# The first attention-scale group of a DiT block: one added by a ones matmul, four VectorE products straight from PSUM, and a new order of the opening

## The chip, the cores and the metric

The kernel runs on one core of a Trainium2 chip. The metric is the device time of one execution in microseconds. Before the change it is 243.63 us, the median of five runs (243.14 to 243.85). All window times below count from the first instruction of the profiled execution.

## The reference

A diffusion-transformer block on 2 batches of 256 tokens with 1152 features. A conditioning vector `c` gives six modulation vectors; the layer-normed input is scaled and shifted, goes through attention with two heads, is gated and added back, and then the same is done around an MLP.

```python
mod = (_silu(c) @ w_mod).reshape(B, 6, 1, D)
shift_a, scale_a, gate_a, shift_m, scale_m, gate_m = [mod[:, i] for i in range(6)]
h = _layernorm(x, axis=-1) * (1 + scale_a) + shift_a
qkv = (h @ wqkv).reshape(B, N, 3, H, Dh)
q, k, v = (qkv[:, :, 0].copy(), qkv[:, :, 1].copy(), qkv[:, :, 2].copy())
attn = _softmax(jnp.einsum('bqhd,bkhd->bhqk', q, k) * Dh ** (-0.5), axis=-1)
a = jnp.einsum('bhqk,bkhd->bqhd', attn, v).reshape(B, N, D) @ wo
x = x + gate_a * a
h2 = _layernorm(x, axis=-1) * (1 + scale_m) + shift_m
m = _gelu(h2 @ w_fc1) @ w_fc2
return x + gate_m * m
```

The change concerns only `(1 + scale_a)` and the product with the layer-normed `x`.

## The kernel before

The 512 tokens are four token tiles of 128 (tiles 0 and 1 are batch 0, tiles 2 and 3 batch 1). The 1152 features are nine chunks of 128, counted by `k`. Activations that feed a matmul lie transposed, features on partitions, tokens along the free dimension: `hT0[:, k, tokens]` (in the trace it is part of `big`). The K projection is built first, chunk by chunk: `k_step(k, c0, c1)` (L288) multiplies chunk `k` of the tokens `c0` to `c1` with six column blocks of `w_k`, one matmul each, and adds into six PSUM accumulators `pk`. A step on one token tile is six matmuls with 128 columns, on two tiles six with 256, on all tiles six with 512.

What a step needs comes through four engines:

- VectorE gathers the statistics of a token tile (`stats_piece`, L188 and L193; for tile 1 ScalarE does it, L203), ScalarE takes the square root (`sqrt1`, L219), VectorE the reciprocal (`recip1`, L222) and then normalizes the tile in two pieces (`norm1`, L235): columns up to CUT = 512, which are the first four chunks, and the other 640 later. The result is `xn`.
- TensorE transposes 128x128 blocks of `xn` into PSUM tiles `pt` (L266 in `transpose_x`, L358 in `transpose_into`).
- The scale comes by `scale_group(g)`: the loads of the scale columns are split into four groups, KGROUPS = chunks 0-1, 2-3, 4-5 and 6-8. For each chunk nine matmuls (L248) with two columns, one for each batch, add up in a PSUM tile `pm`. `add_one` then writes `scale_a` to SBUF with one added, on VectorE (L256) or ScalarE (L258, with the tile `one_t` as bias).
- `modulate` multiplies a transposed block in PSUM with its chunk's scale, read per partition from SBUF, and writes `hT0`, on VectorE (L273) or ScalarE (L275). The shift is added later.

The tiles `pc`, `pt` and `pm` take turns in two PSUM banks, so a new one waits until the earlier content of its bank has been read. Every engine works through its instructions in the order in which the Python code issues them: the last loop of the kernel ties each instruction to the one before it on its engine. So the opening is a schedule written out by hand. `warm(n, pwarm)` (L171) issues matmuls on zeros whose result nobody reads. SyncE issues all loads in one queue: `x`, then in turn a scale group and the chunks of `w_k` that belong to it, then the other weights. In the profiled execution the last packet of scale group 0 lands at 8.85 us, of `w_k` chunk 0 at 9.37, chunk 1 at 9.95, scale group 1 at 11.94, `w_k` chunk 2 at 12.46 and chunk 3 at 13.02.

The opening's order on TensorE around the change is: transposes of tile 0's chunks 0 and 1, four warm matmuls, the 18 scale matmuls of group 0, one warm matmul, six transposes (tile 1's chunks 0 and 1, chunks 2 and 3 of both tiles), `k_step` 0 and 1 on tile 0 and then on tile 1, two transposes of tile 2, the 18 scale matmuls of group 1, `k_step` 0 and 1 on tile 2, `k_step` 2 on tiles 0 and 1. ScalarE scales tile 0's two chunks and later tile 2's; VectorE scales tile 1's, and chunks 2 and 3 of tiles 0 and 1.

Of the kernel before, what the change touches and what calls it, by code (L numbers as in the profile page):

```python
# [8 lines left out]
FP32 = mybir.dt.float32  # L9
BF16 = mybir.dt.bfloat16  # L10
ACT = mybir.ActivationFunctionType
# [8 lines left out]
def kernel(  # L20
# [11 lines left out]
    nc = tc.nc  # L32
    B, N, D = x.shape
# [3 lines left out]
    P = 128  # L37
    T = B * N
    NT = T // P
    TPB = N // P  # L40
    KD = D // P
# [3 lines left out]
    NPD = D // PW  # L45
# [6 lines left out]
    const = ctx.enter_context(tc.tile_pool(name="const", bufs=1))  # L52
# [6 lines left out]
    def acc_tile(shape, name, dt=FP32):  # L59
        return psum.tile(shape, dt, name=name, tag="acc", bufs=6)  # L60

    def aux_tile(shape, name, dt=FP32):
        return psum.tile(shape, dt, name=name, tag="aux", bufs=2)
# [25 lines left out]
    ident = const.tile([P, P], BF16, name="ident")  # L89
    make_identity(nc, ident[:])  # L90
    eps_t = const.tile([P, 1], FP32, name="eps_t")
    nc.vector.memset(eps_t[:], LN_EPS)  # L92
    one_t = const.tile([P, 1], FP32, name="one_t")
    nc.vector.memset(one_t[:], 1.0)
    SW = 32
    sT = act.tile([P, KD, SW], BF16, name="sT")
    nc.gpsimd.memset(sT[:], 0.0)
# [1 line left out]
    KGROUPS = [(0, 2), (2, 4), (4, 6), (6, 9)]  # L99
# [59 lines left out]
    hT0 = aT  # L159
# [9 lines left out]
    def warm(n, dst):  # L169
        for _ in range(n):  # L170
            nc.tensor.matmul(dst[:], zeros[:, 0:P], zeros[:], start=True, stop=True)  # L171
# [12 lines left out]
    xns = [work.tile([P, D], BF16, name="xn", tag="xn", bufs=4) for _ in range(NT)]  # L184
    stats1 = [small.tile([P, NPD, 6], FP32, name="stats1", tag="stats1") for _ in range(NT)]

    def stats_piece(t, j, aggregate=True):
        nc.vector.bn_stats(stats1[t][:, j, :], x_sb[:, t, j * PW:(j + 1) * PW])  # L188
        if j == NPD - 1 and aggregate:
            stats_aggregate(t)  # L190

    def stats_aggregate(t):
        nc.vector.bn_aggr(mv1[:, t, :], stats1[t][:].rearrange("p a b -> p (a b)"))  # L193
# [24 lines left out]
    def sqrt1(t):  # L218
        nc.scalar.activation(rstd1[:, t:t + 1], mv1[:, t, 1:2], ACT.Sqrt, bias=eps_t[:], scale=1.0)  # L219

    def recip1(t, with_nb=False):
        nc.vector.reciprocal(rstd1[:, t:t + 1], rstd1[:, t:t + 1])  # L222
        if with_nb:
            nc.vector.scalar_tensor_tensor(
                nb1[:, t:t + 1], mv1[:, t, 0:1], -1.0, rstd1[:, t:t + 1], op0=ALU.mult, op1=ALU.mult
            )

    def norm1(t, c0, c1, eng):
        if eng == "a":
            nc.scalar.activation(  # L230
                xns[t][:, c0:c1], x_sb[:, t, c0:c1], ACT.Identity,
                bias=nb1[:, t:t + 1], scale=rstd1[:, t:t + 1],
            )
        else:
            nc.vector.tensor_scalar(  # L235
                xns[t][:, c0:c1], x_sb[:, t, c0:c1], mv1[:, t, 0:1], rstd1[:, t:t + 1],
                op0=ALU.subtract, op1=ALU.mult,
            )


    scale_a = act.tile([P, KD, B], FP32, name="scale_a")

    def scale_group(g):
        k0, k1 = KGROUPS[g]
        pm = aux_tile([P, k1 - k0, B], "pm")
        for j in range(k0, k1):
            for k in range(KD):
                nc.tensor.matmul(  # L248
                    pm[:, j - k0, :], w_scale_a[:, k, j * P:(j + 1) * P], sT[:, k, 0:B],
                    start=(k == 0), stop=(k == KD - 1),  # L250
                )

        def add_one(eng):
            dst = scale_a[:, k0:k1, :]
            if eng == "d":
                nc.vector.tensor_scalar_add(dst, pm[:], 1.0)  # L256
            else:
                nc.scalar.activation(dst, pm[:], ACT.Identity, bias=one_t[:])  # L258

        return add_one  # L260

    def transpose_x(ks, ts, pt=None, js=None):
        pt = aux_tile([P, len(ks), len(ts) * P], "pt", BF16) if pt is None else pt
        for i, k in enumerate(ks):
            for j, t in enumerate(ts) if js is None else zip(js, ts):
                nc.tensor.transpose(pt[:, i, j * P:(j + 1) * P], xns[t][:, k * P:(k + 1) * P], ident[:])  # L266
        return pt

    def modulate(pt, i, k, t0, j0, w, eng):
        b = t0 // TPB  # L270
        dst, src, sc = hT0[:, k, t0 * P:t0 * P + w], pt[:, i, j0:j0 + w], scale_a[:, k, b:b + 1]
        if eng == "d":
            nc.vector.tensor_scalar_mul(dst, src, sc)  # L273
        else:
            nc.scalar.mul(dst, src, sc)  # L275
# [8 lines left out]
    def k_step(k, c0=0, c1=T, m0=0, m1=KM1):  # L284
        for m in range(m0, m1):
            if k == 0 and c0 == 0:
                pk[m] = acc_tile([P, T], "pk")
            nc.tensor.matmul(  # L288
                pk[m][:, c0:c1], w_k[:, k, m * P:(m + 1) * P], hT0[:, k, c0:c1],
                start=(k == 0 and c0 == 0), stop=(k == KD - 1), skip_group_check=True,  # L290
            )
# [39 lines left out]
    CUT = 4 * P  # L331
# [7 lines left out]
    recip1(0)  # L339
    norm1(0, 0, CUT, "d")  # L340
    stats_piece(2, 1)
    pt_0 = transpose_x([0, 1], [0])
    warm(4, pwarm)
    act_stats_finish()
    sqrt1(T_ACT)
# [1 line left out]
    recip1(1)  # L347
    norm1(1, 0, CUT, "d")
    stats_aggregate(2)
    norm1(0, CUT, D, "d")  # L350
    scale_group(0)("a")
    for k in range(2):
        modulate(pt_0, k, k, 0, 0, P, "a")
    warm(1, pwarm)
    pt_1 = aux_tile([P, 1, 8 * P], "pt", BF16)

    def transpose_into(pt, slot, k, t):
        nc.tensor.transpose(pt[:, 0, slot * P:(slot + 1) * P], xns[t][:, k * P:(k + 1) * P], ident[:])  # L358

    for k in range(2):  # L360
        transpose_into(pt_1, k, k, 1)
    for k in (2, 3):
        for t in range(TPB):
            transpose_into(pt_1, 2 * (k - 1) + t, k, t)
    for k in range(2):
        modulate(pt_1, 0, k, 1, k * P, P, "d")
    sqrt1(2)
    k_step(0, 0, P)
    k_step(1, 0, P)
    stats_piece(3, 0)  # L370
    recip1(2)
    norm1(2, 0, CUT, "d")
    k_step(0, P, N)
    k_step(1, P, N)
    stats_piece(3, 1)
    stats_piece(3, 2)
    for k in range(2):
        transpose_into(pt_1, 6 + k, k, 2)
    for k in range(2):
        modulate(pt_1, 0, k, 2, (6 + k) * P, P, "a")  # L380
    scale_group(1)("a")
    sqrt1(3)
    for k in (2, 3):
        modulate(pt_1, 0, k, 0, 2 * (k - 1) * P, N, "d")
    k_step(0, N, N + P)
    k_step(1, N, N + P)
    recip1(3)
    norm1(3, 0, CUT, "d")
    k_step(2, 0, N)
    k_step(3, 0, N, 0, 3)  # L390
    pt_4 = transpose_x([0, 1], [3])
    for k in range(2):
        modulate(pt_4, k, k, 3, 0, P, "d")
    k_step(3, 0, N, 3, KM1)
    norm1(1, CUT, D, "d")
    pt_5 = transpose_x([2, 3], [2, 3])
    for i, k in enumerate((2, 3)):
        modulate(pt_5, i, k, 2, 0, N, "a")
    norm1(2, CUT, D, "d")
    norm1(3, CUT, D, "d")  # L400
    add2 = scale_group(2)
    k_step(0, N + P, T)
    k_step(1, N + P, T)
# [46 lines left out]
    for k in range(KD):  # L450
        for b in range(B):
            dst, src = hT[:, k, b * N:(b + 1) * N], hT0[:, k, b * N:(b + 1) * N]
# [56 lines left out]
    for k in range(KD):  # L509
        for m in range(KM1):  # L510
            nc.tensor.matmul(  # L511
                pq[m][:], w_q[:, k, m * P:(m + 1) * P], hT[:, k, :],
                start=(k == 0), stop=(k == KD - 1),
            )
    for m in range(KD):
        if m >= KM1:
            pq.append(acc_tile([P, T], "pacc"))
            for k in range(KD):
                nc.tensor.matmul(
                    pq[m][:], w_q[:, k, m * P:(m + 1) * P], hT[:, k, :],  # L520
                    start=(k == 0), stop=(k == KD - 1),
# [10 lines left out]
    for b in range(B):  # L532
        for h in range(H):
            scores[b, h] = acc_tile([P, TPB, N], "ps_s")
            for qt in range(TPB):
                q0 = b * N + qt * P
                for i in range(HC):
# [3 lines left out]
                        start=(qt == 0 and i == 0), stop=False, skip_group_check=True,  # L541
                    )
    for b in range(B):
        for qt in range(TPB):
            q0 = b * N + qt * P
            for h in range(H):
# [3 lines left out]
                    start=False, stop=True, skip_group_check=True, tile_position=(h * HP, 0),  # L550
# [309 lines left out]
    for gi, (n, t, c0, cw) in enumerate(groups):  # L860
        b = t // TPB
        last = gi == len(groups) - 1
        pacc = acc_tile([P, cw], "pacc")
        for kk in range(KF):
            j, r = divmod(n * KF + kk, 27)
# [3 lines left out]
                start=(kk == 0), stop=(kk == KF - 1),  # L869
# [11 lines left out]
    for ins in list(nc.cur_bb.bb.instructions)[first_traced:]:  # L881
        eng = ins.engine
# [38 lines left out]
```

## Time and profile before

| | |
|---|---|
| device time of the profiled execution | 243.63 us |
| its span, first to last instruction | 241.9 us |
| median of five runs | 243.63 us |
| granted TensorE clock, mean | 1.000 |
| 0 to 9.85 us | TensorE busy 8.41, VectorE 5.12, ScalarE 6.46 us |
| 9.85 to 15.80 us | TensorE busy 5.69, VectorE 4.67, ScalarE 2.25 us |
| 15.80 to 33.50 us | TensorE busy 17.56, VectorE 6.62, ScalarE 4.84 us |
| 33.50 to 98.60 us | TensorE busy 64.88, VectorE 40.59, ScalarE 29.67 us |
| 98.60 us to the end | TensorE busy 139.85, VectorE 36.41, ScalarE 26.29 us |

The page gives busy time and share of each engine (PE is TensorE's matmuls, PEld its weight loads, DVE VectorE, ACT ScalarE, POOL GpSimd, SP SyncE, a q behind the name its sequencer). A line of the timeline gives the start, the duration from the first start to the last end, engine, line, operation, output and input, shape and count of a run of equal instructions, and in brackets the idle time before them and what ended it. The duration of a TensorE matmul counts to its modelled end, which lies behind the start of the next one; how fast matmuls follow each other is read from their starts.

### The profile page before, as it was taken

Reading aid. Unit: us, or ns where it says so; the run is one execution under the profiler, and the core shown is the slowest. Engines: PE = TensorE matmul, PEld = TensorE weight load, DVE = VectorE, ACT = ScalarE, POOL = GpSimd, SP = SyncE. Lnnn points to the kernel's source line nnn. Section 1 sums busy time; section 2 is a strip of 40 time slices with the busy share of each in tenths; the row PEclk is TensorE's granted clock in tenths of the full one; section 3 lists DMA queues with packets and bytes.
Section 4 is the critical chain, followed back from the end, with each engine's and each line's share of the span. In section 5 each row is a group of like instructions: output and inputs, shape, how many; then the busy total and the mean of one; then the engine's idle time right before and its main releaser. Section 6 shows DMA issues by size and latency. Waiting matters only on the chain.

```text
span 241.9 us, 4031 instructions
## 1 busy us (share of the span) xinstructions
PE 236.4 (98%) x1698; PEld 143.1 (59%) x1698; DVE 93.4 (39%) x209; ACT 69.5 (29%) x138; POOL 31.9 (13%) x48
## 2 busy tenths in 40 slices
PE   8999999999999999999999999999999999999994
PEld 2595444466656666888844444444666566665673
DVE  3772450665694676620000029999002000000001
ACT  6532240543736074782222233322000000000000
POOL 1000400000310616200000000000314111111111
PEclk9999999999999999999999999999999999999999
DMA  6999999999999999799999999995891000000000
GB/s 230 322 332 360 378 345 245 339 368 280 253 323 362 379 253 211 202 211 327 328 327 260 200 289 328 326 326 164 264 273 33 19 16 16 20 21 26 18 19 16
DMA packets 76989, 54.48 MB, mean 225 GB/s; under 512 B 26011, under 2 KB 72491, under 8 KB 76971
## 3 DMA queue, kind: packets, MB, share of 16 engines
q1 hardware_dynamic: 76240, 53.02, 77.5%
q0 software_dynamic: 704, 1.20, 1.6%
q8 instruction: 13, 0.21, 0.4%
q14 instruction: 5, 0.04, 0.1%
q10 hardware_dynamic: 27, 0.00, 0.0%
HBM read 46.90 MB, written 1.19 MB: 199 GB/s over the span
## 4 chain that ended last, share of the span: by engine, by line
PE 58%; ACT 2%; DMA 1%; issue 0%; DVE 0%; ACTq 0%; DVEq 0%
PE pacc L866 29%; PE pacc L802 29%; ACT hT L687 2%; DMA hT<-xn 1%; ACT xn L666 0%; ACT rstd L657 0%; DVE tmp L872 0%; DVE o_sb L874 0%; ACTq L687 0%; DVEq L872 0%
## 5 line engine op out<-in xcount | busy, mean ns | idle before, releaser
L802 PE MATMUL pacc<-hT,w_f 128*128 128x256 bf16 (+1 forms) x432 | 70.5, 326 | 0.2 <-ACT hT L687 0.2
L866 PE MATMUL pacc<-w_f,gT 128*128 128x384 bf16 (+2 forms) x468 | 70.5, 314 | 0.0
L866 PEld LDWEIGHTS <-gT 128*128 128x128 bf16 x468 | 44.4, 98 | 26.3
L802 PEld LDWEIGHTS <-w_f 128*128 128x128 bf16 x432 | 42.2, 98 | 28.1 <-issue 0.4
L485 DVE SCALAR_TENSOR_TENSOR late<-w_gate_mT,late 128x1152 bf16<-128x1152 bf16 x18 | 24.4, 1357 | 36.2 <-DMA w_gate_mT<-in_w_mod_dram 35.7
L872 DVE TENSOR_TENSOR tmp<-pacc,gate 128x384 f32<-128x384 f32 (+2 forms) x13 | 6.8, 526 | 62.7 <-PE pacc L866 50.8
L840 ACT ACTIVATE gT<-pacc 128x512 bf16<-128x512 f32 x24 | 14.3, 597 | 32.3 <-PE pacc L802 32.3
L485 DVE SCALAR_TENSOR_TENSOR s_spill<-w_scale_m,s_b 128x1152 bf16<-128x1152 bf16 x12 | 16.3, 1357 | 8.6 <-DMA w_scale_m<-in_w_mod_dram 8.2
L874 POOL TENSOR_TENSOR o_sb<-tmp,x 128x384 bf16<-128x384 f32 (+1 forms) x12 | 11.6, 973 | 47.7 <-DVE tmp L872 47.7
L705 PE MATMUL pacc<-w_o,big 128*128 128x384 bf16 (+2 forms) x117 | 17.9, 314 | 0.0
L584 PE MATMUL pacc<-w_v,hT 128*128 128x384 bf16 x108 | 17.9, 326 | 0.0
L705 PEld LDWEIGHTS <-big 128*128 128x128 bf16 x117 | 11.0, 98 | 6.8 <-ACT big L627 0.2
L584 PEld LDWEIGHTS <-hT 128*128 128x128 bf16 x108 | 10.4, 98 | 7.0 <-issue 0.2
L288 PE MATMUL pk<-big,w_k 128*128 128x128 bf16 (+2 forms) x102 | 13.3, 279 | 0.0
L711 POOL TENSOR_TENSOR x<-tmp,x_sb 128x384 f32<-128x384 f32 (+1 forms) x11 | 9.8, 888 | 17.4 <-DVE tmp L710 9.6
L511 PE MATMUL pacc<-hT,w_q 128*128 128x512 bf16 x54 | 11.8, 379 | 0.1
L327 POOL DMA_DIRECT2D gates_dram<-grow x4 | 2.1, 519 | 70.6 <-DVE grow L826 70.6
L818 ACT ACTIVATE gT<-pacc 128x512 bf16<-128x512 f32 x12 | 6.9, 595 | 10.3 <-PE pacc L802 10.2
L288 PEld LDWEIGHTS <-w_k 128*128 128x128 bf16 x102 | 7.7, 98 | 3.0
L511 PEld LDWEIGHTS <-w_q 128*128 128x128 bf16 x54 | 5.3, 98 | 6.7 <-issue 0.4
L171 PE MATMUL pwarm<-zeros 128*128 128x512 bf16 x21 | 7.9, 533 | 1.2 <-DVE eps_t L92 1.2
L710 DVE TENSOR_TENSOR tmp<-pacc,gate 128x384 f32<-128x384 f32 (+2 forms) x13 | 6.7, 522 | 5.4 <-PE pacc L705 5.2
(101 smaller groups left out, 159.4 us busy)
## 6 DMA issues: line engine op xcount, KB each, us to landing
w_f<-in_w_fc_dram SPq DMA_DIRECT2D x14, 864.0 KB, 10.9
w_f<-in_w_fc_dram SPq DMA_DIRECT2D x2, 2592.0 KB, 10.5
w_f<-in_w_fc_dram SPq DMA_DIRECT2D x2, 1728.0 KB, 13.7
w_shift_a<-in_w_mod_dram SPq DMA_DIRECT2D x3, 864.0 KB, 10.6
w_v<-in_wqkv_dram SPq DMA_DIRECT2D x3, 864.0 KB, 6.0
w_gate_a<-in_w_mod_dram SPq DMA_DIRECT2D x3, 864.0 KB, 9.2
w_o<-in_wo_dram SPq DMA_DIRECT2D x3, 864.0 KB, 6.1
w_shift_m<-in_w_mod_dram SPq DMA_DIRECT2D x3, 864.0 KB, 13.0
```

The source lines that it names most:

```text
L171: nc.tensor.matmul(dst[:], zeros[:, 0:P], zeros[:], start=True, stop=True)
L288: nc.tensor.matmul(pk[m][:, c0:c1], w_k[:, k, m * P:(m + 1) * P], hT0[:, k, c0:c1], start=(k == 0 and c0 == 0), stop=(k == KD - 1), skip_g ...
L485: nc.vector.scalar_tensor_tensor(spill, wT[:, j, :], 1.0, s_b[b], op0=ALU.mult, op1=ALU.mult, accum_out=dst(j, b),)
L511: nc.tensor.matmul(pq[m][:], w_q[:, k, m * P:(m + 1) * P], hT[:, k, :], start=(k == 0), stop=(k == KD - 1),)
L584: nc.tensor.matmul(pacc[:], hT[:, k, t * P:(t + 1) * P], w_v[:, k, pnl * PW:(pnl + 1) * PW], start=(k == 0), stop=(k == KD - 1),)
L705: nc.tensor.matmul(pacc[:], aT[:, k, t * P:(t + 1) * P], w_o[:, k, c0:c1], start=(k == ks[0]), stop=(k == ks[-1]),)
L711: (nc.vector if (t, i) in ((1, 2), (3, 3)) else nc.gpsimd).tensor_tensor(x1[:, t, c0:c1], tmp[:], x_sb[:, t, c0:c1], op=ALU.add)
L802: nc.tensor.matmul(dst, w_f1[m // KD][:, k, ml * P:(ml + 1) * P], hT[:, k, c0:c1], start=(k == 0), stop=(k == KD - 1),)
L818: nc.scalar.activation(gT[:, ms[0]:ms[-1] + 1, b * N:(b + 1) * N], pacc[:], ACT.Gelu_apprx_tanh)
L840: nc.scalar.activation(gT[:, m, :], pacc[:], ACT.Gelu_apprx_tanh)
L866: nc.tensor.matmul(pacc[:], gT[:, kk, t * P:(t + 1) * P], w_f2[j][:, r, c0 - n * PW:c0 - n * PW + cw], start=(kk == 0), stop=(kk == KF - 1),)
L874: (nc.vector if last else nc.gpsimd).tensor_tensor(o_sb[:], tmp[:], x1[:, t, c0:c0 + cw], op=ALU.add)
```

## The change

- `one_t` goes. A row of 128 ones (`ones_r`, one partition, bf16) takes its place.
- `scale_group` is split in `scale_group_matmuls` and `scale_group_copy`. The matmuls of each of the four groups are headed by one matmul of `ones_r` with itself, which sets every sum in `pm` to one; the scale matmuls add to it, so none of them starts a sum. What reads `pm` is then a plain copy.
- For group 0, tile 0's and tile 1's transposed chunks 0 and 1 lie in one PSUM tile `pt_0`, and VectorE makes all four products, with the scale read straight from `pm_0` in PSUM. ScalarE copies `pm_0` to `scale_a` for later use by batch 1.
- The order of the opening changes. Tile 1's two transposes follow the group-0 scale matmuls at once. The square root of tile 2 is taken before the copy; VectorE normalizes tile 2 right behind the four products and takes the statistics of tile 3 behind that in one piece. The four transposes of chunks 2 and 3 stand between `k_step` 0 and 1 on tile 1. The group-1 scale matmuls move from before to behind `k_step(0)` on tile 2, and `k_step(1)` on tile 2 follows them. ScalarE instead of VectorE scales chunks 2 and 3 of tiles 0 and 1, with tile 3's square root between the two. VectorE normalizes the rest of tile 0 (`norm1(0, CUT, D)`) later, in front of the same piece of tile 1.

```diff
-    one_t = const.tile([P, 1], FP32, name="one_t")
-    nc.vector.memset(one_t[:], 1.0)
+    ones_r = const.tile([1, P], BF16, name="ones_r")
+    nc.vector.memset(ones_r[:], 1.0)
...
-    def scale_group(g):
+    def scale_group_matmuls(g):
         k0, k1 = KGROUPS[g]
         pm = aux_tile([P, k1 - k0, B], "pm")
+        nc.tensor.matmul(
+            pm[:].rearrange("p j b -> p (j b)"), ones_r[:, 0:P], ones_r[:, 0:(k1 - k0) * B], start=True, stop=False,
+            skip_group_check=True,
+        )
         for j in range(k0, k1):
             for k in range(KD):
                 nc.tensor.matmul(
                     pm[:, j - k0, :], w_scale_a[:, k, j * P:(j + 1) * P], sT[:, k, 0:B],
-                    start=(k == 0), stop=(k == KD - 1),
+                    start=False, stop=(k == KD - 1), skip_group_check=True,
                 )
 
-        def add_one(eng):
+        return pm
+
+    def scale_group_copy(g, pm):
+        k0, k1 = KGROUPS[g]
+
+        def copy_out(eng):
             dst = scale_a[:, k0:k1, :]
             if eng == "d":
-                nc.vector.tensor_scalar_add(dst, pm[:], 1.0)
+                nc.vector.tensor_copy(dst, pm[:])
             else:
-                nc.scalar.activation(dst, pm[:], ACT.Identity, bias=one_t[:])
...
+    def scale_group(g):
+        return scale_group_copy(g, scale_group_matmuls(g))
...
-    pt_0 = transpose_x([0, 1], [0])
+    def transpose_into(pt, slot, k, t):
+        nc.tensor.transpose(pt[:, slot * P:(slot + 1) * P], xns[t][:, k * P:(k + 1) * P], ident[:])
+
+    pt_0 = aux_tile([P, 4 * P], "pt", BF16)
+    for k in range(2):
+        transpose_into(pt_0, k, k, 0)
     warm(4, pwarm)
...
     stats_aggregate(2)
-    norm1(0, CUT, D, "d")
-    scale_group(0)("a")
+    sqrt1(2)
+    pm_0 = scale_group_matmuls(0)
     for k in range(2):
-        modulate(pt_0, k, k, 0, 0, P, "a")
+        transpose_into(pt_0, 2 + k, k, 1)
+    for t in range(TPB):
+        for k in range(2):
+            nc.vector.tensor_scalar_mul(
+                hT0[:, k, t * P:(t + 1) * P], pt_0[:, (2 * t + k) * P:(2 * t + k + 1) * P], pm_0[:, k, 0:1]
+            )
+    nc.scalar.copy(scale_a[:, 0:2, :], pm_0[:])
     warm(1, pwarm)
-    pt_1 = aux_tile([P, 1, 8 * P], "pt", BF16)
...
-    for k in range(2):
-        transpose_into(pt_1, k, k, 1)
+    recip1(2)
+    norm1(2, 0, CUT, "d")
+    pt_1 = aux_tile([P, 8 * P], "pt", BF16)
+    k_step(0, 0, P)
+    k_step(1, 0, P)
+    for j in range(NPD):
+        stats_piece(3, j)
+    k_step(0, P, N)
     for k in (2, 3):
         for t in range(TPB):
             transpose_into(pt_1, 2 * (k - 1) + t, k, t)
-    for k in range(2):
-        modulate(pt_1, 0, k, 1, k * P, P, "d")
-    sqrt1(2)
-    k_step(0, 0, P)
-    k_step(1, 0, P)
-    stats_piece(3, 0)
-    recip1(2)
-    norm1(2, 0, CUT, "d")
-    k_step(0, P, N)
     k_step(1, P, N)
-    stats_piece(3, 1)
-    stats_piece(3, 2)
     for k in range(2):
         transpose_into(pt_1, 6 + k, k, 2)
     for k in range(2):
-        modulate(pt_1, 0, k, 2, (6 + k) * P, P, "a")
-    scale_group(1)("a")
-    sqrt1(3)
+        nc.scalar.mul(hT0[:, k, N:N + P], pt_1[:, (6 + k) * P:(7 + k) * P], scale_a[:, k, 1:2])
+    k_step(0, N, N + P)
+    pm_1 = scale_group_matmuls(1)
+    nc.scalar.copy(scale_a[:, 2:4, :], pm_1[:])
     for k in (2, 3):
-        modulate(pt_1, 0, k, 0, 2 * (k - 1) * P, N, "d")
-    k_step(0, N, N + P)
-    k_step(1, N, N + P)
+        nc.scalar.mul(hT0[:, k, 0:N], pt_1[:, 2 * (k - 1) * P:2 * k * P], scale_a[:, k, 0:1])
+        if k == 2:
+            sqrt1(3)
     recip1(3)
     norm1(3, 0, CUT, "d")
+    k_step(1, N, N + P)
     k_step(2, 0, N)
     k_step(3, 0, N, 0, 3)
     pt_4 = transpose_x([0, 1], [3])
     for k in range(2):
         modulate(pt_4, k, k, 3, 0, P, "d")
     k_step(3, 0, N, 3, KM1)
+    norm1(0, CUT, D, "d")
     norm1(1, CUT, D, "d")
```

More of the change, by code (lines that the diff above doesn't have):

```diff
@@ L249, in scale_group @@
                     pm[:, j - k0, :], w_scale_a[:, k, j * P:(j + 1) * P], sT[:, k, 0:B],
-                    start=(k == 0), stop=(k == KD - 1),
+                    start=False, stop=(k == KD - 1), skip_group_check=True,
                 )
-        def add_one(eng):
+        return pm
+    def scale_group_copy(g, pm):
+        k0, k1 = KGROUPS[g]
+        def copy_out(eng):
             dst = scale_a[:, k0:k1, :]
             if eng == "d":
-                nc.vector.tensor_scalar_add(dst, pm[:], 1.0)
+                nc.vector.tensor_copy(dst, pm[:])
             else:
-                nc.scalar.activation(dst, pm[:], ACT.Identity, bias=one_t[:])
-        return add_one
+                nc.scalar.copy(dst, pm[:])
+        return copy_out
+    def scale_group(g):
+        return scale_group_copy(g, scale_group_matmuls(g))
     def transpose_x(ks, ts, pt=None, js=None):
@@ L349 @@
     stats_aggregate(2)
-    norm1(0, CUT, D, "d")
-    scale_group(0)("a")
+    sqrt1(2)
+    pm_0 = scale_group_matmuls(0)
     for k in range(2):
-        modulate(pt_0, k, k, 0, 0, P, "a")
-    warm(1, pwarm)
-    pt_1 = aux_tile([P, 1, 8 * P], "pt", BF16)
-    def transpose_into(pt, slot, k, t):
-        nc.tensor.transpose(pt[:, 0, slot * P:(slot + 1) * P], xns[t][:, k * P:(k + 1) * P], ident[:])
-    for k in range(2):
-        transpose_into(pt_1, k, k, 1)
+        transpose_into(pt_0, 2 + k, k, 1)
[5 more added lines that the diff above has]
+    nc.scalar.copy(scale_a[:, 0:2, :], pm_0[:])
+    warm(1, pwarm)
+    recip1(2)
[6 more added lines that the diff above has]
+    k_step(0, P, N)
     for k in (2, 3):
```

## The prediction

> **What bounds the kernel now.** I read the page's first two parts, then the waits, then the timeline, first from 0 to 14 us and then in slices narrow enough to show single matmuls.
>
> ```profile
> PE 236.4 (98%) x1698; PEld 143.1 (59%) x1698; DVE 93.4 (39%) x209; ACT 69.5 (29%) x138; POOL 31.9 (13%) x48
> ...
> PEclk9999999999999999999999999999999999999999
> ```
>
> TensorE is the bound. Busy time hides short stalls, because a matmul's pipelined tail counts as busy, so I compare starts: neighbouring 128-column matmuls start 0.056 us apart (24 of them from 10.25 to 11.59), 256-column ones 0.109, the 2-column scale matmuls 0.025. What starts later than that is a stall.
>
> ```profile
> 8.89 0.60 PE L248 MATMUL pm<-sT,w_scale_a 128*128 128x2 bf16 x18
> 9.54 0.26 ACT L258 ACTIVATE scale_a<-pm,one_t 128x4 f32<-128x4 f32 x1 [1.27 <-PE pm L248]
> 9.83 0.62 ACT L275 ACTIVATE big<-pt,scale_a 128x128 bf16<-128x128 bf16 x2
> 9.85 0.49 PE L358 MATMUL pt<-ident,xn 128*128 128x128 bf16 x6
> 10.25 1.50 PE L288 MATMUL pk<-big,w_k 128*128 128x128 bf16 x24
> 11.50 0.41 DVE L235 TENSOR_SCALAR xn<-x_sb,mv,rstd 128x512 bf16<-128x512 bf16 x1
> 11.97 0.28 PE L358 MATMUL pt<-ident,xn 128*128 128x128 bf16 x2 [0.22 <-DVE xn L235]
> 12.09 0.59 PE L248 MATMUL pm<-sT,w_scale_a 128*128 128x2 bf16 x18
> 12.29 0.62 ACT L275 ACTIVATE big<-pt,scale_a 128x128 bf16<-128x128 bf16 x2 [1.65 <-PE pt L358]
> ```
>
> The reader is to see two chains. At 9.54 ScalarE adds one, scales, and lets the K matmuls start at 10.25. At 12.29 it scales token tile 2 while TensorE works through the 18 scale matmuls of group 1, placed there as filler. By starts, TensorE's stalls from 9.36 to 13.51 are 0.27 (before 9.85), 0.07 (10.25), 0.38 (11.97, waiting for VectorE's norm), 0.17 (12.71) and 0.13 (before the 256-wide step at 13.51): 1.02 us in all. After 16 us the only stalls over 0.1 us are 0.30 at 33.48 and 0.38 at 98.56; both end chains that TensorE's own results start (the waits name ScalarE L687 for the second, never a load). So later stages move with TensorE, and a us here is a us at the end.
>
> **What the Trainium skill says.** "TensorEngine Tiling (Array Packing)", Key Properties: changing the tiling mode drains TensorE. The ones matmul contracts over one row, so it is built with a 32-row tile, between 128-row ones. The trace agrees where a 64-row tile is entered and left:
>
> ```profile
> 54.34 0.27 PE L539 MATMUL ps_s<-big 128*128 128x256 bf16 x1
> 54.54 0.39 PE L548 MATMUL ps_s<-big 64*128 64x256 bf16 x4
> ```
>
> From 54.34 to 54.54 is 0.205 where 0.109 is normal: 0.095 lost on entry, and again on leaving (54.88 to 55.09). The one small row-tile there is, the transpose of c, agrees for the exit:
>
> ```profile
> 3.01 0.19 PE L174 MATMUL pc<-ident,c_sb 18*128 18x18 bf16 x1
> 3.13 0.61 PE L171 MATMUL pwarm<-zeros 128*128 128x512 bf16 x1
> ```
>
> "VectorE: DVE Perf Modes", Scalar operands, allows a per-partition scalar operand and names no extra price; no row of before has one in PSUM. "PSUM — Partial Sum Buffer", PSUM bank collisions, says two engines must not touch one bank at once; so ScalarE's copy out of the scale's bank is made to wait for VectorE's four products. It has over 1 us to spare.
>
> **The change, part by part.** I follow TensorE's order in the changed program.
>
> (1) Head. The ones matmul of group 0 sits in the stall before the load's arrival at 8.89: nothing (0.1 if leaving its tile costs after the load has landed). The 18 end at 9.36; tile 1's two transposes follow at 9.36 and 9.42, and the last ends at 9.42+0.22=9.64 (xn of tile 1 is ready at 8.98). VectorE starts 0.04 later, as it does after L266 (14.54+0.22 to 14.80). Its 0.38 us norm of tile 0's tail, which ran at 9.04, has moved away. First product 9.68 to 9.96, K matmuls 0.05 later (as from 11.91 to the load at 11.96): 10.01 instead of 10.25, **−0.24**. The products come every 0.20 us (L273), the matmuls of one step take 0.33, so none waits again. The PSUM scalar: at least 0, at most 0.10 (half a step); I take 0.
>
> (2) Tile 2 comes earlier. VectorE is free at 10.48 and sqrt1(2) has run; reciprocal 0.18, norm 0.41: 11.07, not 11.91. TensorE does 24 matmuls (1.34) and four transposes (0.22): tile 2's transposes at 11.57 instead of 11.97, **−0.40** by here.
>
> (3) The filler is gone. Group 1's scale matmuls now stand behind k_step(0,N,N+P). The second transpose ends at 11.63+0.22=11.85; ScalarE starts 0.10 later (this wait goes through an extra semaphore instruction, as 15.31 to 15.41), and from its start to the matmul takes 0.42 (12.29 to 12.71): 12.37. TensorE was free at 11.69, so a **0.68 us stall** replaces 0.38+0.17.
>
> (4) k_step(0,N,N+P) to 12.70. Then the ones matmul: 0.095 in, 0.025, 0.095 out, that is **0.215**; nothing covers it. The 18 from 12.92 to 13.37, k_step(1,N,N+P) to 13.70. Their result goes through ScalarE in series, copy and then the 256-wide product. Before, from the last scale matmul's start (9.34) to the product's start (9.83) was 0.49: 13.34+0.49=13.83. To the matmul 0.42, plus 0.11 for 256 columns (0.48 against 0.37): 14.36. A **0.66 us stall**, where before VectorE's product let the step start at 13.51. k_step(2,0,N) is now 0.85 late. Check by stalls: now 0.32 (before 10.01), 0.68, 0.66 and 0.19 for the switches, 1.85 against 1.02, plus 0.025 of matmul: 0.85.
>
> (5) The rest. The second product starts 0.37+0.25 after the first (sqrt1(3) between), ends near 14.92 and is in time for 15.01. pm_2's ones matmul waits for VectorE anyway (0.18 at 15.33): entry hidden, 0.12 added, 0.97. Group 3's is bare: 0.215, **1.19**. The moved norm adds 0.36 to VectorE's row at about 16.0; it ends near 17.6, before the transposes at about 18.1: nothing, and only 0.5 us further on would it cost. ScalarE's copies replace adds of the same size. SP's and POOL's orders are unchanged; the loads' waits stay where they were, and a later TensorE has more slack on them.
>
> Sum: +1.19 us. The profiled execution took 243.63 us (span 241.9 and 1.7 around it), which is also the median: **244.8 us**.
>
> **The rivals.**
> (A) The switch is nearly free for so small a matmul: less 0.19, 0.095 and 0.19, so +0.72, 244.3. For: the c transpose shows only the exit, at a time when matmuls still start at half the later rate (0.43 us for 512 columns, later 0.22). Against: the 64-row rows.
> (B) More than I count: the PSUM scalar (0.10), the drain in (1) (0.1), transposed loads around 90 us landing worse: +1.4 to +1.7, 245.2. For: one such transfer takes 3.5 us there, beside other loads. Against: they are issued from TensorE's progress and shift with it.
> (C) Part is absorbed: if the wait at 98.56 hung on loads by the clock, up to 0.38 would vanish: 244.4. Against: the chain of waits.
> (D) Faster: TensorE reaches tile 2's transposes 0.40 early, and the two ScalarE hand-overs cost no more than they do now. This would need the stalls of (3) and (4), switches included, under 0.70 us (0.17+0.13+0.40) where I count 1.54; with them at 0.30 it is 243.2. For: ScalarE is idle then and could be quicker than its rows. Against: each hand-over is a sum of measured steps, with nothing left on TensorE to cover it.
>
> **How the numbers follow.** Chances: forecast 0.52 (its own range 244.5 to 245.1), A 0.20, B 0.13, C 0.07, D 0.06, the rest unknown. From 244.0 (A, the hand-overs 0.3 shorter) to 245.4 (B) leaves out D and the tails. A measurement tells about 0.2%, 0.49 us, from no change, so "same" ends at 244.1: only the low end of A and C and half of D lie within. Faster 0.05, same 0.11, slower 0.84.
>
> **What would show it.** K matmuls from 10.0; tile 2's transposes near 11.6; a TensorE stall of 0.6 to 0.7 behind them, named after ScalarE, and a second before the 256-wide step near 14.4; about 0.1 either side of each ones matmul; the last matmul 1.2 later. It is wrong if the 256-wide step starts before 13.8, or if the 1.2 us shrink between 16 and 100 us.

## The result, and the profile after

The changed kernel takes 244.49 us, the median of 43 runs (244.2 to 245.5), beside 243.69 us for the kernel before (80 runs): a ratio of 1.0034 with a 95% interval of 1.0028 to 1.0040, about 0.8 us slower. The forecast was 1.2 us slower, with a range from 244.0 to 245.4.

The page of the changed kernel, span and first part:

```profile
span 242.7 us, 4039 instructions
...
PE 236.8 (98%) x1702; PEld 143.2 (59%) x1702; DVE 93.5 (39%) x209; ACT 69.5 (29%) x138; POOL 31.9 (13%) x48
```

The span grew by 0.8 us; the four ones matmuls are there (1702 against 1698), and TensorE's busy time tells nothing of the loss. The loss is in starts. The timeline of the changed kernel, 8.5 to 14.4 us (start, duration, engine, line, operation, output and input, and in brackets the idle time before and what ended it):

```profile
8.62 0.17 PE L246 MATMUL pm<-ones_r 1*128 1x4 bf16 x1
8.87 0.60 PE L252 MATMUL pm<-sT,w_scale_a 128*128 128x2 bf16 x18
...
9.33 0.27 PE L355 MATMUL pt<-ident,xn 128*128 128x128 bf16 x2
...
9.64 0.88 DVE L373 TENSOR_SCALAR big<-pt,pm 128x128 bf16<-128x128 bf16 x4 [0.51 <-PE pt L355]
9.98 1.17 PE L300 MATMUL pk<-big,w_k 128*128 128x128 bf16 x18 [0.17 <-DVE big L373]
...
11.54 0.28 PE L355 MATMUL pt<-ident,xn 128*128 128x128 bf16 x2
11.92 0.62 ACT L393 ACTIVATE big<-pt,scale_a 128x128 bf16<-128x128 bf16 x2 [1.15 <-PE pt L355]
12.33 0.49 PE L300 MATMUL pk<-big,w_k 128*128 128x128 bf16 x6 [0.52 <-ACT big L393]
...
12.76 0.17 PE L246 MATMUL pm<-ones_r 1*128 1x4 bf16 x1
12.87 0.60 PE L252 MATMUL pm<-sT,w_scale_a 128*128 128x2 bf16 x18
13.33 0.49 PE L300 MATMUL pk<-big,w_k 128*128 128x128 bf16 x6
13.51 0.16 ACT L396 COPY scale_a<-pm 128x4 f32<-128x4 f32 x1 [0.97 <-PE pm L252]
13.70 0.47 ACT L398 ACTIVATE big<-pt,scale_a 128x256 bf16<-128x256 bf16 x1
...
14.23 0.38 PE L300 MATMUL pk<-big,w_k 128*128 128x256 bf16 x2 [0.40 <-ACT big L398]
```

Read down TensorE's starts. The K matmuls begin at 9.98 instead of 10.25, and tile 2's transposes at 11.54 instead of 11.97: so far the kernel is 0.43 us ahead. The second transpose starts at 11.60 and should be followed at 11.65; the next matmul starts at 12.33, when ScalarE's product is there: 0.68 us of stall. Then 0.10 is lost in front of the ones matmul and 0.08 behind it. The second stall is 0.56: the step on tile 2 would have been followed at 13.66, the 256-wide step starts at 14.23. Before it started at 13.51, so 0.72 us are lost here. At the Q projection it is 1.03 us (34.51 against 33.48), at the end of the wait near 98.6 only 0.8. Here are these two places, first in the kernel before (the first line is of its timeline, the others are of its chain of waits: start, duration, what), then in the chain of the changed kernel:

```profile
33.48 0.38 PE L511 MATMUL pacc<-hT,w_q 128*128 128x512 bf16 x1
...
90.65 3.53 DMA hT<-xn
...
98.56 69.59 PE pacc L802 x425
```

```profile
34.51 11.82 PE pacc L527 x54
...
99.38 69.60 PE pacc L818 x425
```

The page sums each chain up by engine, first that of the kernel before, then that of the changed one:

```profile
PE 58%; ACT 2%; DMA 1%; issue 0%; DVE 0%; ACTq 0%; DVEq 0%
```

```profile
PE 94%; DMA 3%; DVE 1%; ACT 0%; SPq 0%; issue 0%; DVEq 0%; ACTq 0%
```

Before, the chain that ended last went back from the first MLP matmuls to ScalarE, to the transposed load of normed rows (`DMA hT<-xn`) and so away from TensorE. Now it stays on TensorE all the way to the load of scale group 0. Something at 90 us that used to hold the kernel holds it less. Whether that is the missing 0.2 us is what e4 to e9 ask.

### The profile page after: what moved, and what is told of

The parts are those of the page before. It is cut to its first block, busy times and chain, and to the rows that moved or that the text cites. A ratio compares the mean times of both kernels' runs of the same rounds, so it can differ in the third digit from the quotient of the medians.

```text
span 242.7 us, 4039 instructions
## 1 busy us (share of the span) xinstructions
PE 236.8 (98%) x1702; PEld 143.2 (59%) x1702; DVE 93.5 (39%) x209; ACT 69.5 (29%) x138; POOL 31.9 (13%) x48
## 3 DMA queue, kind: packets, MB, share of 16 engines
HBM read 46.90 MB, written 1.19 MB: 198 GB/s over the span
## 4 chain that ended last, share of the span: by engine, by line
PE 94%; DMA 3%; DVE 1%; ACT 0%; SPq 0%; issue 0%; DVEq 0%; ACTq 0%
PE pacc L818 29%; PE pacc L882 29%; PE pacc L721 7%; PE pacc L600 7%; PE pk L300 5%; PE pacc L527 5%; DMA w_scale_a<-in_w_mod_dram 3%; PE pacc L535 2%; PE pk L330 2%; PE pa L635 1%; PE ps_s L555 1%; PE pn L448 1%; PE pm L252 1%; PE pt L278 1%; PE pg L483 1%; SPq L85 0%
## 5 line engine op out<-in xcount | busy, mean ns | idle before, releaser
L890 POOL TENSOR_TENSOR o_sb<-tmp,x 128x384 bf16<-128x384 f32 (+1 forms) x12 | 11.6, 972 | 48.2 <-DVE tmp L888 48.2
```

Of the source, the lines that this page charges most:

```text
L890: (nc.vector if last else nc.gpsimd).tensor_tensor(o_sb[:], tmp[:], x1[:, t, c0:c0 + cw], op=ALU.add)
```

## The experiments

### What the order costs: e1

Group 1's scale matmuls go back in front of the step on tile 2.

```diff
-    k_step(0, N, N + P)
     pm_1 = scale_group_matmuls(1)
     nc.scalar.copy(scale_a[:, 2:4, :], pm_1[:])
+    k_step(0, N, N + P)
```

> The changed kernel with one move undone: the 18 scale matmuls of group 1 (with their ones matmul) and the copy stand again before k_step(0) on tile 2. Theory (the loss is ScalarE's two hand-overs with nothing on TensorE beside them): the first stall of 0.68 us is filled by the ones matmul and the 18 (0.66), k_step(0) on tile 2 still starts near 12.33, the step on chunk 2 near 13.2 instead of 14.23, about 1.0 us earlier; the median falls to 243.5 to 243.8, near the kernel before. Rival (the ones matmuls' tile switches are the loss): the order does not matter, the ones matmuls are all still there, the median stays at 244.3 to 244.5.

Measured: 243.83 us, ratio to before 1.0009 (0.9995 to 1.0024). TensorE's timeline of e1 from 11.6 us, and then two lines of ScalarE's:

```profile
11.82 0.28 PE L355 MATMUL pt<-ident,xn 128*128 128x128 bf16 x2
12.02 0.17 PE L246 MATMUL pm<-ones_r 1*128 1x4 bf16 x1
12.24 0.60 PE L252 MATMUL pm<-sT,w_scale_a 128*128 128x2 bf16 x18
12.71 1.49 PE L300 MATMUL pk<-big,w_k 128*128 128x128 bf16 x16
```

```profile
12.88 0.16 ACT L395 COPY scale_a<-pm 128x4 f32<-128x4 f32 x1
13.08 0.47 ACT L398 ACTIVATE big<-pt,scale_a 128x256 bf16<-128x256 bf16 x1
```

The stall behind the transposes is filled: ones matmul and the 18 run while ScalarE scales tile 2, and the step follows at 12.71 with no wait for ScalarE. In this execution the first scale matmul started 0.27 us later than in the changed kernel (9.14 against 8.87, when the load landed), so I count from it: the 256-wide step starts 4.46 us behind it (13.60), in the changed kernel 5.36, before 4.61. The move is worth 0.90 us there, and with it the ratio is back near one. The rival, by which order does not matter, falls. The median lies just above the expected 243.5 to 243.8: TensorE now gets to group 1's scale matmuls so early that it waits about 0.12 us for their weights, which landed at 12.20.

### What the tile switch costs: e2

The ones matmul contracts over 128 rows of 1/128 instead of one row of 1. The sum is the same, the tile is that of its neighbours.

```diff
-    ones_r = const.tile([1, P], BF16, name="ones_r")
-    nc.vector.memset(ones_r[:], 1.0)
+    ones_r = const.tile([P, P], BF16, name="ones_r")
+    nc.vector.memset(ones_r[:], 1.0 / P)
+    ones_c = const.tile([P, 8], BF16, name="ones_c")
+    nc.vector.memset(ones_c[:], 1.0)
...
-            pm[:].rearrange("p j b -> p (j b)"), ones_r[:, 0:P], ones_r[:, 0:(k1 - k0) * B], start=True, stop=False,
+            pm[:].rearrange("p j b -> p (j b)"), ones_r[:, 0:P], ones_c[:, 0:(k1 - k0) * B], start=True, stop=False,
```

> The changed kernel with the ones matmul over 128 rows of 1/128 instead of one row of 1, so that no tiling mode changes. Theory (the switch is the price): the gaps of 0.08 to 0.10 on both sides of each ones matmul go, 0.18 for group 1, 0.07 for group 2, 0.18 for group 3, 0.43 us in all; what is left of each is 0.025; median 244.0 to 244.2. Rival (an extra matmul into the same PSUM bank costs this whatever its shape): gaps and median stay, 244.4 to 244.6.

Measured: 244.12 us, ratio to before 1.0013 (1.0004 to 1.0023). TensorE's timeline of e2 from 12.4 us:

```profile
12.49 0.50 PE L302 MATMUL pk<-big,w_k 128*128 128x128 bf16 x6 [0.52 <-ACT big L395]
12.83 0.17 PE L248 MATMUL pm<-ones_c,ones_r 128*128 128x4 bf16 x1
12.86 0.59 PE L254 MATMUL pm<-sT,w_scale_a 128*128 128x2 bf16 x18
13.31 0.49 PE L302 MATMUL pk<-big,w_k 128*128 128x128 bf16 x6
```

From the step's first matmul to the first scale matmul it is 0.37 us here and 0.54 in the changed kernel. The ones matmul itself now takes 0.03. From the first scale matmul to the Q projection it is 25.19 us against 25.64: 0.45 for three groups, where 0.43 was expected. An extra matmul is nearly free (0.03 us); the change of the row count is what costs.

### Group 0's part alone: e3

Groups 1 to 3 get their one from an add again, the filler is back, VectorE scales chunks 2 and 3. The core of the edit to the changed kernel:

```diff
-    k_step(0, N, N + P)
-    pm_1 = scale_group_matmuls(1)
-    nc.scalar.copy(scale_a[:, 2:4, :], pm_1[:])
+    scale_group(1)("a")
+    sqrt1(3)
     for k in (2, 3):
-        nc.scalar.mul(hT0[:, k, 0:N], pt_1[:, 2 * (k - 1) * P:2 * k * P], scale_a[:, k, 0:1])
-        if k == 2:
-            sqrt1(3)
+        nc.vector.tensor_scalar_mul(hT0[:, k, 0:N], pt_1[:, 2 * (k - 1) * P:2 * k * P], scale_a[:, k, 0:1])
+    k_step(0, N, N + P)
     recip1(3)
```

> Group 0's part of the change alone: ones matmul, one PSUM tile and four VectorE products for group 0, with tile 2's norm right behind them; groups 1 to 3 get their one from an add as before, group 1's scale matmuls stand before k_step(0) on tile 2, VectorE scales chunks 2 and 3. Theory (the head gains, the rest loses): tile 2's transposes near 11.55, the step on chunk 2 near 13.15 against 13.51 before, nothing lost later: 0.3 to 0.4 us faster than before, 243.2 to 243.4. Rival (the products from PSUM and the regrouped order of VectorE lose too): 243.7 or more.

Measured: 243.56 us, ratio 0.9992 (0.9980 to 1.0005): no gain that can be told. In the profiled execution (243.81 us, above the median) the opening is where it was expected: the 256-wide step at 13.16, the Q projection at 33.13, 0.34 us ahead of before. But near 98.6 TensorE stalls twice, 0.54 and 0.38 us, where before it stalls once for 0.38, and then it is 0.18 us behind. The expectation was a miss, and one thing that it missed is again the place at 90 us.

The other is in the opening. Group 0's load landed at 8.14 us here and at 8.85 in the profile of before, so not all of the 0.34 us comes from the edit. Counted from the first scale matmul (8.38), the 256-wide step starts 4.78 us later, in the kernel before 4.61: in this execution TensorE waits 0.29 us for VectorE, which is not through with tile 1, and 0.36 for group 1's load, the longer of the two waits of this line (us in total, times, longest):

```profile
PEld L278 <- DMA w_scale_a<-in_w_mod_dram: 0.6, 2, 0.4
```

### A pure delay: e4

```diff
     pt_5 = transpose_x([2, 3], [2, 3])
+    for _ in range(6):
+        transpose_x([2, 3], [2, 3], pt_5)
```

> The kernel before with 24 transposes of four blocks repeated into the same PSUM tile at about 15 us: work added that changes no result, a pure delay of TensorE. They take 1.34 us, of which 0.18 fills the wait that stands behind them at 15.33: 1.16 us at 33 us. Theory (a part of any delay is given back at the wait at 98.56, where the transposed load of tile 1's normed rows took 3.31 instead of 3.53 us in the changed kernel): 0.9 to 1.0 us slower at the end, 244.6 to 244.7, with that load shorter than 3.53 us and the wait at about 0.2 instead of 0.38. Rival (the shorter load was chance of one execution): 1.1 to 1.2 us slower, 244.8 to 244.9, wait 0.38.

Measured: 244.46 us, ratio 1.0031 (1.0020 to 1.0043), 0.8 us for 1.16 us of delay. Counted from the first scale matmul, the Q projection is 1.16 us later than before (25.74 against 24.58), the first matmul behind the wait near 99.6 only 0.91 (90.58 against 89.67): the wait is 0.14 instead of 0.38. A delay that has nothing to do with the change is shortened at the same place, as the theory has it; the loss at the end is even a little less than it expected.

### What sits there: e5 to e9

Tile 1's normed rows are transposed by a load; six ScalarE products wait for it, the first MLP matmuls wait for those. The issue of that load and the first of the products, in the timelines of before and of the changed kernel:

```profile
90.65 1.50 SPq L676 DMA_TRANSPOSE hT<-xn  x1
94.29 3.06 ACT L687 ACTIVATE hT<-hT,shift_m,scale_m 128x256 bf16<-128x256 bf16 x6 [3.66 <-DVE stats L717]
```

```profile
91.69 1.30 SPq L692 DMA_TRANSPOSE hT<-xn  x1
95.10 3.06 ACT L703 ACTIVATE hT<-hT,shift_m,scale_m 128x256 bf16<-128x256 bf16 x6 [3.44 <-DMA hT<-xn]
```

From issue to product: 3.64 us before, 3.41 after. The stage table of the kernel before (window, length, busy time and count of each engine, clock, DMA share, GB/s) says what is going on:

```profile
87.00:88.00 1.00, 1.00 (x26) 0.70 (x26) 0.97 (x3) 1.00 (x4) 0.00 (x0) 1.00 1.11 329
88.00:89.00 1.00, 1.00 (x27) 0.60 (x16) 0.09 (x1) 1.00 (x4) 0.00 (x0) 1.00 1.14 311
89.00:90.00 1.00, 1.00 (x8) 0.61 (x7) 0.76 (x4) 0.47 (x2) 0.00 (x0) 1.00 2.23 93
```

Weights are moved at 311 to 329 GB/s until about 89 us, and the first transposed load (tile 0's) is issued at 87.08 into that. e7 is the kernel before with one of those weight loads issued later:

```diff
     load_f1(0, 0)
-    load_f1(0, 1)
...
     ln2_transpose(1)
+    load_f1(0, 1)
     load_f1(0, 2)
```

> The kernel before with one load moved: the second panel of the first MLP weight (864 KB) is issued behind the transposed load of tile 1 and not ahead of it; nothing else. Theory: the transposed loads find the DMA engines idle, take 3.2 to 3.3 us instead of 3.53, the wait at 98.56 falls from 0.38 to 0.15 or less, 0.2 to 0.3 us faster, 243.3 to 243.45. Rival (the wait hangs on TensorE's own results alone, as the prediction had it): the same time as before, 243.6 to 243.7. It is also possible that the moved panel comes late for the MLP's fourth block at about 101 us, which would show as a new wait on a load there.

Measured: 243.47 us, ratio 0.9992 (0.9983 to 1.0000): its median is 0.15 us under before's, just above the expected 243.3 to 243.45, and the interval reaches up to no change at all. The profile is plainer. The stage table of e7, and then the load and the product:

```profile
86.00:87.00 1.00, 1.00 (x12) 0.89 (x10) 0.96 (x3) 1.00 (x2) 0.00 (x0) 1.00 0.14 41
87.00:88.00 1.00, 1.00 (x28) 0.71 (x29) 0.97 (x3) 1.00 (x3) 0.00 (x0) 1.00 0.04 12
```

```profile
90.58 1.30 SPq L675 DMA_TRANSPOSE hT<-xn  x1
93.95 3.06 ACT L686 ACTIVATE hT<-hT,shift_m,scale_m 128x256 bf16<-128x256 bf16 x6 [3.40 <-DMA hT<-xn]
```

The weights are through before the rows are ready, the load takes 3.37 us to the product, and TensorE's stall is 0.14 instead of 0.38, with TensorE where it was before. Nothing waits for the moved panel.

e5 is the kernel before once more, in one execution.

> The kernel before once more, one execution with its trace, to see how far single executions differ. Theory (the transposed load of tile 1's normed rows, issued at 90.65 us, queues behind weight loads that go by the clock of the DMA engines and end at about 91 us): it takes 3.4 to 3.7 us again and the wait before the first matmul on it is 0.3 to 0.45. Rival (3.53 against 3.31 us was chance): any value between 3.2 and 4.1.

Measured: from issue (90.54) to product 3.83 us, 0.19 more than in the first profile; to the landing it is 3.73, just above the expected 3.4 to 3.7. The stall of 0.38 is there again, with a further 0.21 ahead of it.

e9 is the changed kernel with e7's edit.

> The changed kernel, as it is, with e7's one moved load. Theory (the changed kernel loses about 1.0 us in its opening, and 0.2 of that is given back only because the kernel before waits longer for the loads ahead of its transposed rows): with the panel out of the way nothing is left to give back. In the changed kernel the wait is already at its floor (0.18), so the moved load brings it nothing: 244.35 to 244.55, that is 0.9 to 1.05 us behind e7 (243.47). Rival (the moved load helps for another reason): it gains 0.2 or more here too, 244.2 or less.

Measured: 244.55 us, ratio 1.0036 (1.0021 to 1.0050). The moved load brings the changed kernel nothing, as its load already took 3.41 us; here it is 3.39. Beside e7's 243.47 the change costs 1.08 us, close to what its opening loses (1.03 at the Q projection; between the single traces of e9 and e7 it is 1.23).

All twelve profiles together, those of e6, e8 and e10 below with them. "Flat out until" is where the DMA engines first fall under half of their 326 GB/s for half a microsecond; a load is issued by SyncE and has landed when its last packet has; all figures are us:

| run | flat out until | tile 0's load issued | and landed | tile 1's landed behind it | tile 1's issue to product | stall of TensorE |
|---|---|---|---|---|---|---|
| before | 89.2 | 87.1 | 93.29 | 0.89 | 3.64 | 0.38 |
| e5, before again | 89.2 | 87.0 | 93.38 | 0.89 | 3.83 | 0.21 + 0.38 |
| e3, 0.34 ahead at the Q projection | 89.2 | 86.7 | 93.44 | 0.91 | 4.16 | 0.54 + 0.38 |
| e6, 0.39 behind there | 90.0 | 87.5 | 94.21 | 0.92 | 4.18 | 0.56 + 0.38 |
| after | 89.0 | 88.1 | 93.70 | 1.29 | 3.41 | 0.18 |
| e4, delay | 90.0 | 88.4 | 92.84 | 2.42 | 3.38 | 0.14 |
| e1 | 89.2 | 87.5 | 93.31 | 1.02 | 3.37 | 0.13 |
| e2 | 89.5 | 87.8 | 93.64 | 1.04 | 3.40 | 0.15 |
| e7, panel later | 86.0 | 87.0 | 91.65 | 2.19 | 3.37 | 0.14 |
| e9, after with panel later | 86.2 | 88.2 | 92.81 | 2.29 | 3.39 | 0.15 |
| e8, panel later | 86.0 | 86.9 | 90.97 | 2.71 | 3.37 | 0.12 |
| e10, panel later | 86.2 | 87.1 | 91.68 | 2.27 | 3.37 | 0.13 |

In the first four rows the second load lands 0.89 to 0.92 us behind the first, and in no row closer. In the other eight it lands 3.26 to 3.31 us after its own issue. So in the first four rows the second load was held up behind the first, and the first took long: 6.2 to 6.7 us from issue to landing, beside 5.6 to 5.8 in after, e1 and e2, and 4.1 to 4.7 where the weights were through (e7 to e10). All twelve traces fit this reading, but no run moves the first load alone to test it.

Two things stay open. The end of the weights is not fixed by the clock: it is at 89.0 to 89.2 in five runs whose tile 0 is issued anywhere from 86.7 to 88.1, yet later, at 90.0, in e4 and e6. And in e4 the first load took only 4.4 us although it was issued 1.6 us ahead of that end, where e1 and e2, at about 1.7, took 5.8.

### A better opening, and a version that beats both: e6, e8, e10

e6 takes e2's ones matmul and e3's order. e8 and e10 (the same kernel twice) are e6 with e7's load.

> The changed kernel with the ones matmul over 128 rows, group 1's scale matmuls back before k_step(0) on tile 2 and VectorE scaling chunks 2 and 3: all of the opening's gains and none of its losses. The step on chunk 2 should start 0.35 to 0.45 us before that of the kernel before, and the Q projection 0.3 to 0.4 us before it (33.1). Theory (the first normed rows cannot land before about 94.2 us, whatever TensorE does, for the loads ahead of them): the transposed load takes 3.9 to 4.1 us, the wait behind it grows by 0.3, and the end is within 0.15 us of before: 243.5 to 243.7. Rival (a gain in the opening is a gain at the end): 243.2 to 243.3.

> Both together: the opening of e6 and the moved panel of e7. Theory: with the loads out of the way the opening's 0.3 to 0.4 us reach the end, in sum 0.55 to 0.7 us faster than before, 242.9 to 243.1. Rival (something else by the clock holds the rows): no better than e7, 243.3 or more.

> e8 once more, beside e9 on the same chip: 242.9 to 243.3, faster than before by 0.1 to 0.25%.

Measured: e6 243.67 us, ratio 1.0007 (0.9995 to 1.0020); e8 243.10, 0.9982 (0.9972 to 0.9991); e10 243.18, 0.9984 (0.9975 to 0.9993). So e6 gains nothing, and e8 is faster than the kernel before by 0.16 to 0.18%, 0.4 to 0.5 us, in both of its measurements. The moved load, worth some 0.15 us to the kernel before and nothing to the changed one, is worth 0.5 to 0.6 to e6 (243.67 against 243.10 and 243.18): the earlier TensorE arrives, the more the place at 90 us takes from it.

The gain is a little less than was expected of e8 (0.55 to 0.7), and the traces show one reason. Two waits of e6's TensorE timeline, near 12 and 20 us, and its sum of waits for these loads (us in total, times, longest; the longest is the one for group 0):

```profile
12.26 0.38 PE L254 MATMUL pm<-sT,w_scale_a 128*128 128x2 bf16 x9
...
20.32 0.33 PE L254 MATMUL pm<-sT,w_scale_a 128*128 128x2 bf16 x7 [0.19 <-DMA w_scale_a<-in_w_mod_dram]
```

```profile
PEld L254 <- DMA w_scale_a<-in_w_mod_dram: 1.9, 4, 1.1
```

TensorE lost 0.27 and 0.33 us here, in front of groups 1 and 3. e10's trace shows the same two waits (0.29 and 0.46), e3's the first (0.36), e8's none. Group 1's load was not late of itself: it landed 3.08 us behind group 0's (9.13 and 12.21), in the profile of before 3.09 behind it (8.85 and 11.94). But the kernel before starts group 1's matmuls 3.20 us behind its first scale matmul and so has only about 0.1 us in hand, while e6 reaches them after 2.82. So the faster opening runs into the load stream, and its lead at the 256-wide step, counted from the first scale matmul, is 0.28 us (4.33 against 4.61; 0.26 in e10) and not 0.35 to 0.45. In e8 there is no such lead (4.62), as VectorE was late with tile 1 and TensorE waited 0.47 us for it.

e6's profiled execution took 244.58 us and was the slowest of its 14, so its trace tells little of its median. Group 0's load landed late in it, and its 256-wide step starts at 13.50, level with before's 13.51; its Q projection is at 33.87, where 33.1 was expected. The median, 243.67, lies inside the expected band.

## Why the prediction was right, and where it was off

**Direction, place and cause** were right. Both stalls of parts (3) and (4) are there with ScalarE named, the first to the hundredth (0.68). e1 shows the order's part (0.90 us at the 256-wide step), e2 the switches' part (0.45).

**Part (1), the head.** −0.24 forecast, −0.27 measured; 0.03 of that is the earlier arrival of group 0's load in that execution. The scale read from PSUM costs nothing that shows: the four products start at 9.64 and take 0.88 us together, 0.20 apart, like those with the scale in SBUF.

**Part (2).** −0.40 forecast, −0.43 measured, the same 0.03 included.

**Part (4), one term too large.** ScalarE's copy was priced like the add it replaces ("adds of the same size"), 0.26 us. It takes 0.16. So the second stall is 0.56 and not 0.66. The switch cost 0.10 on entry and 0.08 on leaving, against 0.095 each. With the head's 0.03 this makes the 0.72 us at the 256-wide step where the prediction has 0.85.

**Part (5).** For groups 2 and 3 together 0.34 forecast; from the 256-wide step to the Q projection the changed kernel takes 20.28 us against 19.97: 0.31. VectorE's moved norm delayed nothing.

**"A us here is a us at the end"** is the step that failed, for about 0.2 us of the 1.0. The prediction took the wait at 98.56 to hang on TensorE's own results alone and held rival C, a part absorbed there, at 0.07. It read who TensorE waits for, and that is ScalarE; one step further back the chain of the kernel before names the load of 3.53 us shown above, and rival B, which mentions it, lets it shift with TensorE. C was right in kind: the transposed rows wait behind transfers that do not move one for one with TensorE. Its "up to 0.38" was 0.20, since 0.12 to 0.18 of that wait is there in every trace in which tile 1's load is not held up. That the 0.2 us belong to this place is shown by e4, by e7 with e9, and by e8 beside e6; that it is tile 0's load that holds tile 1's is read from the traces alone. Rival A is refuted by e2, rival B's extra costs did not appear, rival D by the stalls themselves.

**The sum as it should have been:** 1.19 less 0.10 (copy), 0.03 (load), 0.03 (switches) gives 1.03 at the Q projection, less 0.2 at 98.6 gives 0.8. All four lie on the same side, so none hid another.

## What to carry to other kernels

A block of small matmuls that looks like mere preparation can be the filler that hides another engine's hand-over; before moving it, write down what TensorE does between a transpose and the first use of its scaled result. A helper matmul should have the row count of its neighbours: ones over 128 rows of 1/128 instead of one row took about 0.17 us out of a place where nothing covers it (0.54 to 0.37 from the step to the scale matmuls). And before carrying a gain or loss from an early stage to the end, look behind every later wait for transfers that do not move with the engine, because those can give back part of a delay and eat part of a gain. The same holds close by: an opening can be made faster only down to the landing of its next load, so set the start of each block beside the landing of what it reads.

## What the runs showed of the hardware that was not expected

- ScalarE's copy of 128x4 fp32 from PSUM took 0.16 us, its activation with a bias tile on the same shape 0.26.
- A per-partition scalar in PSUM was as cheap for VectorE as one in SBUF: 0.28 us for one product, 0.20 from start to start.
- A one-row matmul with four columns between 128-row ones lost 0.10 us in front and 0.07 to 0.08 behind.
- Issuing the transposed loads of tiles 0 and 1 took SyncE 1.43 to 2.04 us in the profiles of before, e3, e5 and e6, in which the second load landed late, and 1.25 to 1.30 in the other eight.
- The transposed loads of tiles 0 and 1, issued 3.6 us apart, never landed closer than 0.89 us to each other in the twelve profiles.
- The same first load of scale weights, in kernels with the same load order at the start, landed between 8.14 and 9.13 us in the twelve profiled executions, and at 8.85 and 8.47 in the two of the kernel before.
